# The end of a forward scan: weights issued early, six stores behind the rows, O and P in the V buffers, GLU buffers laid out anew

## The chip, the cores and the metric

The kernel runs as one program on one core of one Trainium2 chip. Five engines with queues of their own matter here: TensorE (PE; its weight loads are listed apart as PEld), VectorE (DVE), ScalarE (ACT), GpSimd (POOL) and SyncE (SP), which issues transfers only. Transfers are issued from queues too: SP's (SPq in the trace) and GpSimd's are those of interest. All of them are carried out by 16 DMA engines, between the memory outside (HBM) and the core's SBUF. The metric is the device time of one execution in microseconds (us); lower is better.

## The reference

One layer with two blocks under a condition vector, forward and backward: the output and eleven gradients. Block A is a recurrent attention, walked in 64 segments of 32 rows with 8 memory rows ahead of each; block B is a gated product. D is 512, there are 32 heads of 128, and F is 1792.

```python
for s in range(n_seg):                                   # 64 segments, one after the other
    h = concatenate([mem, xs], axis=1)                   # 8 + 32 rows
    q, k, v = (einsum('btd,dhe->bhte', h, W) for W in (Wq, Wk, Wv))
    p = softmax(where(mask, einsum('bhqe,bhke->bhqk', q, k) * scale, -1e9))
    o = einsum('bhqk,bhke->bhqe', p, v)
    o = einsum('bhte,hed->btd', o, Wo)
    mem = o[:, :M, :]; outs.append(o[:, M:, :])
...
x = x + ga * A(layernorm(x) * (1 + ca) + sa)
h = layernorm(x) * (1 + cb) + sb
x = x + gb * ((sigmoid(h @ w_gate) * (h @ w_up)) @ w_down)
```

## The kernel before

The program is a chain of passes: the forward scan over the 64 stages (segments), then a pass over the gated block (GLU) in 16 tiles of 128 rows, forward and backward at once, then weight gradients of the GLU, then the backward scan from stage 63 down to 0, last the weight gradients of the attention. All passes share one SBUF: a pool of a later pass lies over the buffers of an earlier one, and each first use of a buffer there waits for the last reader or writer of what lay beneath, a store's landing included.

**A stage of the forward scan** (`phase2`, lines 449 to 1163) makes K, Q and V rows (`proj`, `v_chunk`), turns them, makes the scores and their exponentials (`st_exp`, tile ET), the product with V (`pv`), and scales it by 1/sum into the tile Ost (`ost`, L957 on VectorE, L954 on ScalarE). Ost is turned into OT, OT times Wo gives the rows of the stage (`outproj`, at_ps); these are summed (`split_pair`, `sum_pair`) and stored to AOA in HBM by `store_rows` (L347), from GpSimd's queue. Each four stages the memory rows of four stages are worked out together by `TailRows` (ao_tps, ao_b) and stored in `rows_b` (L811). For the backward scan each stage also leaves in HBM: KST and QST (L608, L609), VT (L1154), PS (L1155, the scaled probabilities, tile Pst), OT (L1127) and OSR (L1089, from Ost); these go through SP's queue. ET, Vst and OT have two buffers, taken in turn; Ost, Pst and VTr have one.

**The last stage** (s = 63) has an order of its own. VT and PS are made on TensorE (`turn_v`, `turn_p`) rather than by a transposing transfer, PS is scaled in `scale_p` (L946, VectorE), and the work for tile 0 of the GLU runs in between in nine small steps (`first_tile`). The GLU's three weights are loaded over Wk and Wv from GpSimd's queue as those fall free: w_gate at L996, w_up at L1061, w_down at L1086. Rows of tile 1 are loaded at L995 (`glu_load`, L1188 to L1191), those of tile 0 at the end of the scan, then PS of stage 63 (L1160) and its K and Q rows (`late_rows`).

**The GLU pass** (`phase3`) is a pipeline of seven steps, s0 to s6, run deepest first, so that a tile's step k stands in turn k after the tile began. s0 makes the normed rows, s1 their turned form hdT, s2 gate and up products (L1333, L1337), their sigmoid and u (ScalarE), hh and umh (VectorE); s3 asks SP for the transpose hhT of hh (L1357) and makes du (L1364 on TensorE, L1366 on VectorE) and dg (L1368); s4 multiplies hhT with w_down (L1379); s5 multiplies the transposes of du and dg with the turned weights (L1404). In the first turns TensorE also turns w_down (L1242) and w_gate, w_up (L1231).

Order: every pass is recorded with `pin`, which keeps each engine's and queue's instructions in the order in which they are written; on SP and GpSimd in the scan, transfers stand in that order with the engine's own work. Buffers of the GLU come from the pool `p3s` in the order of their first use.

The edits touch `store_rows`, `rows_b`, `scale_p`, `ost`, `ott_first`, `ott_rest`, the body of the stage loop, its end, and the steps s0 to s5.

## Time and profile before

| | us |
|---|---|
| device time, median of 3 runs | 2972.12 |
| lowest and highest of them | 2970.28, 2975.39 |
| the profiled execution, its own time | 2976.26 |
| its span, first to last instruction | 2974.5 |
| GLU's gate products (L1333), first and last start | 952.1, 1240.4 |
| products with du's transpose (L1404) | 994.7 to 1274.2 |
| last gradient's products (L2300) | 2553.9 to 2971.0 |

All rows of the trace count from the start of the profiled span. TensorE is busy for 2913.0 us of it, 98%. The clock that was granted to it averaged 0.998.

How the views are read. The view of who waited for whom has one row for each pair of waiter and releaser: the sum in us, how often, and the longest. The view of busy time in stretches gives, after the stretch and its length, the busy us and the number of instructions of PE, PEld, DVE, ACT and POOL, then TensorE's clock, the busy share of the DMA engines and GB/s. The view in order of time gives start, length, engine, line, operation, tiles written and read, shapes and the number of merged instructions; in brackets the idle time before it and what ended it. SPq is SP's queue: a row there is the issue of a transfer, and its end is not the transfer's landing. A row in the view of one line gives shortest, median and longest duration in ns. In the view of transfers the last number of a row, where there is one, is the median time in us from issue to landing.

### The profile page before, as it was taken

Reading aid. Unit: us, or ns where it says so; the run is one execution under the profiler, and the core shown is the slowest. Engines: PE = TensorE matmul, PEld = TensorE weight load, DVE = VectorE, ACT = ScalarE, POOL = GpSimd, SP = SyncE. Lnnn points to the kernel's source line nnn. Section 1 sums busy time; section 2 is a strip of 40 time slices with the busy share of each in tenths; the row PEclk is TensorE's granted clock in tenths of the full one; section 3 lists DMA queues with packets and bytes.
Section 4 is the critical chain, followed back from the end, with each engine's and each line's share of the span. In section 5 each row is a group of like instructions: output and inputs, shape, how many; then the busy total and the mean of one; then the engine's idle time right before and its main releaser. Section 6 shows DMA issues by size and latency. Waiting matters only on the chain.

```text
span 2974.5 us, 105438 instructions
## 1 busy us (share of the span) xinstructions
PE 2913.0 (98%) x43838; PEld 1818.8 (61%) x43838; DVE 1625.0 (55%) x3689; ACT 1340.7 (45%) x3234; POOL 1231.7 (41%) x2487
## 2 busy tenths in 40 slices
PE   6999999999998999999999999999999999999999
PEld 3666666666665444445677776777777754445545
DVE  5565565665555788733456665666566632850011
ACT  3666666666665444312355555555555520110011
POOL 2555555545545222221344444444444432762111
PEclk9999999999999999999999999999999999999999
DMA  9889988998899899998699999999999997786565
GB/s 308 221 226 220 219 220 223 219 216 220 211 228 275 210 231 229 239 284 276 193 248 259 246 255 238 253 250 253 252 253 253 250 278 245 250 265 191 161 215 172
DMA packets 838066, 703.01 MB, mean 236 GB/s; under 512 B 537698, under 2 KB 710162, under 8 KB 836692
## 3 DMA queue, kind: packets, MB, share of 16 engines
q1 hardware_dynamic: 711972, 485.29, 66.3%
q0 software_dynamic: 54512, 148.63, 15.9%
q10 hardware_dynamic: 71104, 62.34, 6.5%
q8 instruction: 345, 5.65, 0.8%
q14 instruction: 133, 1.09, 0.1%
HBM read 294.99 MB, written 276.35 MB: 192 GB/s over the span
## 4 chain that ended last, share of the span: by engine, by line
PE 88%; DMA 4%; issue 3%; DVE 2%; ACT 1%; POOL 1%; SPq 0%; DVEq 0%; POOLq 0%; ACTq 0%
PE gps L2300 14%; PE pass_ps L257 14%; PE dh_ps L215 8%; PE g_ps L1923 5%; PE pass_ps L677 5%; PE gps5o L2315 4%; PE dhq_ps L223 4%; PE at_ps L223 4%; PE dh_tps L215 3%; PE gps L1583 3%; PE mm L1404 2%; PE turn_ps L890 2%; PE tps L1840 2%; PE st_ps L900 1%; PE mm L1364 1%
## 5 line engine op out<-in xcount | busy, mean ns | idle before, releaser
L2300 PE MATMUL gps<-rows,hrows 128*128 128x512 bf16 (+2 forms) x2160 | 415.5, 355 | 0.0
L2300 PEld LDWEIGHTS <-hrows 128*128 128x128 bf16 x2160 | 211.1, 98 | 204.5 <-issue 0.9
L1152 POOL TENSOR_TENSOR Pst<-Pst,rden 120x1408 bf16<-120x1408 bf16 x63 | 159.7, 2535 | 344.5 <-issue 209.0
L63 DVE CAST ot<-gps 128x512 bf16<-128x512 f32 (+3 forms) x76 | 48.1, 633 | 308.2 <-PE gps L2300 222.5
L1968 POOL COPY dOst<-RAd 96x512 bf16<-96x512 bf16 x128 | 75.1, 611 | 298.9 <-DVE RAd L63 298.7
L61 ACT ACTIVATE ot<-gps 128x512 bf16<-128x512 f32 (+3 forms) x75 | 41.2, 549 | 348.2 <-PE gps L2300 220.1
L677 PE MATMUL pass_ps<-Wv,hT 128*32 128x512 bf16 (+2 forms) x2304 | 186.8, 357 | 0.0
L2304 POOL DMA_DIRECT2D out_dram<-ot x104 | 78.6, 756 | 255.8 <-DVE ot L63 129.5
L257 PEld LDWEIGHTS <-hT 128*32 128x32 bf16 x4096 | 117.2, 97 | 95.9 <-issue 5.7
L63 DVE CAST Vst<-pass_ps 96x512 bf16<-96x512 f32 x128 | 87.3, 682 | 106.2 <-ACT RBv L61 102.7
L215 PE MATMUL dh_ps<-WvT,dVT 128*32 128x512 bf16 x2048 | 134.5, 383 | 1.7 <-DVE RBd L63 0.2
L223 PE MATMUL at_ps<-Wo,OT 128*32 128x256 bf16 x4096 | 128.1, 276 | 1.3 <-DMA Wo<-in_A_Wo_dram 0.9
L677 PE MATMUL pass_ps<-Wv,hb 128*32 128x512 bf16 (+2 forms) x636 | 126.5, 339 | 0.2
L257 PE MATMUL pass_ps<-Wk,hT 128*32 128x512 bf16 x2048 | 122.7, 380 | 2.1 <-POOL hT L563 1.1
L257 PE MATMUL pass_ps<-WoT,dyT 128*32 128x256 bf16 (+1 forms) x3072 | 122.8, 308 | 1.0 <-ACT dyT L2049 0.9
L257 PE MATMUL pass_ps<-Wq,hT 128*32 128x512 bf16 x2048 | 123.2, 379 | 0.3 <-DVE RBk L63 0.3
L223 PE MATMUL dhq_ps<-WqT,dQT 128*32 128x256 bf16 x4096 | 123.1, 273 | 0.2 <-issue 0.2
L215 PE MATMUL dh_ps<-WkT,dKT 128*32 128x512 bf16 x2048 | 122.3, 380 | 0.0
L2315 PE MATMUL gps5o<-WoT,rows 128*128 128x512 bf16 x560 | 121.0, 379 | 0.0
L223 PEld LDWEIGHTS <-dQT 128*32 128x32 bf16 x4096 | 109.9, 97 | 16.1 <-issue 0.4
L317 DVE TENSOR_TENSOR dST<-dh_ps,dST 128x512 bf16<-128x512 f32 x64 | 44.3, 692 | 130.3 <-ACT dST L316 130.3
L1910 DVE SCALAR_TENSOR_TENSOR dS<-dp_ps,Pst_l 128x480 bf16<-128x480 f32 (+1 forms) x192 | 106.2, 608 | 12.4 <-PE dp_ps L1908 6.7
(480 smaller groups left out, 7040.3 us busy)
## 6 DMA issues: line engine op xcount, KB each, us to landing
OSR<-Ost SPq DMA_DIRECT2D x64, 352.0 KB
OT<-OT SPq DMA_DIRECT2D x64, 352.0 KB
PS<-Pst SPq DMA_DIRECT2D x64, 352.0 KB
Pst_l<-PS SPq DMA_DIRECT2D x64, 352.0 KB
OT_l<-OT SPq DMA_DIRECT2D x64, 352.0 KB
DVR<-rows_x POOLq DMA_DIRECT2D x64, 352.0 KB, 6.0
DKR<-rows_x POOLq DMA_DIRECT2D x64, 352.0 KB, 5.7
DQR<-rows_x POOLq DMA_DIRECT2D x64, 352.0 KB, 3.5
```

The lines of the kernel that those rows point to most:

```text
L63: return nc.vector.tensor_copy(out, in_)
L215: self.nc.tensor.matmul(ps[32 * j:32 * j + 32, :], lhsT=lhsT, rhs=w, start=(n < 4), stop=(n >= total - 4), tile_position=(0, 32 * j))
L223: nc.tensor.matmul(ps[32 * j:32 * j + 32, :], lhsT=x[k], rhs=w[k][:, 256 * d:256 * d + 256], start=(n == 0), stop=(n == total - 1), tile_p ...
L257: self.nc.tensor.matmul(ps[32 * j:32 * j + 32, :], lhsT=lhs(c), rhs=rhs, start=(c == 0), stop=(c == DC - 1), tile_position=(0, 32 * j))
L677: nc.tensor.matmul(ps[32 * j:32 * j + 32, o * E:(o + n) * E], lhsT=lhsT, rhs=wc[:, 3 * a + hl:3 * (a + n - 1) + hl + 1:3, :], start=(c == ...
L1152: nc.gpsimd.tensor_tensor(Pst[0:120, :, :], Pst[0:120, :, :], rden[:, :].unsqueeze(2).to_broadcast([120, G, 128]), op=ALU.mult)
L1583: nc.tensor.matmul(ps[:], lhsT=h2r[:, j, c * 128:(c + 1) * 128], rhs=xr[:, j, :], start=(j == 0), stop=(j == NT - 1))
L1910: nc.vector.scalar_tensor_tensor(out=part3(dS, pi)[:, :, 0:120], in0=ps[:, 0:n, 0:120], scalar=cfg.scale, in1=part3(Pst, pi)[:, :, 0:120], ...
L1923: nc.tensor.matmul(ps[:, j, 0:w], lhsT=lh[:, g * GW:(g + 1) * GW], rhs=rh[:, g * GW:g * GW + w], start=True, stop=True)
L2300: nc.tensor.matmul(ps[:, 0:ng * E], lhsT=hrows[:, tp_, c * 128:(c + 1) * 128], rhs=rows[:, tp_, 0:ng * E], start=(tp_ == 0), stop=(tp_ == ...
L2304: (nc.sync if i == len(todo) - 1 else nc.gpsimd).dma_start(outw[c * 128:(c + 1) * 128, h0:h0 + 3 * (ng - 1) + 1:3, :], ot[:, 0:ng * E].rea ...
L2315: nc.tensor.matmul(pss[gg][:], lhsT=rows[:, t, gg * E:(gg + 1) * E], rhs=dyrows[:, t, :], start=(n == 0), stop=(n == NTP - 1))
```

## The change

- w_up is loaded right behind w_gate, ahead of the scaling of stage 62's Pst on GpSimd; w_down after the third V chunk.
- In stage 63, O is written into the free V buffer (`Orows`, that of the next stage, which does not exist) rather than Ost, and P into the stage's own V buffer, by ScalarE group by group (eleven small scalings with a per-row scale) rather than by three VectorE products.
- The stores of OSR, OT and PS of stages 62 and 63, and VT of 63, move behind the rows: `row_q` sends the last AOA rows through SP's queue, tiles 0 and 2 of the GLU are loaded next, and then the stores follow, in an order with `late_rows`' K and Q among them.
- The GLU's tiles are placed once in a fixed list before the pass (`places`, `buf`), so that the first buffer of each name has a chosen place; the number of buffers of each name stays the same.

```diff
+        self.row_q = nc.gpsimd
...
-                nc.gpsimd.dma_start(dram.rearrange("r (c x) -> (r c) x", x=128), rb[:])
+                self.row_q.dma_start(dram.rearrange("r (c x) -> (r c) x", x=128), rb[:])
...
-                    nc.gpsimd.dma_start(self.AOA[4 * b + i + 1, 32:32 + M, :].rearrange("r (c x) -> (r c) x", x=128),
+                    self.row_q.dma_start(self.AOA[4 * b + i + 1, 32:32 + M, :].rearrange("r (c x) -> (r c) x", x=128),
...
+                Orows = Ost if s < NS - 1 else Vsts[(s + 1) % 2]
...
                 def scale_p(pi):
-                    n = min(PG, G - pi * PG)
-                    nc.vector.tensor_tensor(Pst[0:120, pi * PG:pi * PG + n, :], turned_p[pi][0:120, 0:n, :],
-                                            rden[:, pi * PG:pi * PG + n].unsqueeze(2).to_broadcast([120, n, 128]), op=ALU.mult)
+                    for j in range(min(PG, G - pi * PG)):
+                        g = pi * PG + j
+                        nc.scalar.activation(Vst[0:120, g * GW:(g + 1) * GW], turned_p[pi][0:120, j, :], AF.Copy,
+                                             scale=rden[:, g:g + 1])
...
-                            nc.scalar.activation(Ost[0:120, g * GW:(g + 1) * GW], or_ps[0:120, j, :], AF.Copy,
+                            nc.scalar.activation(Orows[0:120, g * GW:(g + 1) * GW], or_ps[0:120, j, :], AF.Copy,
...
                     nc.gpsimd.dma_start(self.w_gate, io["B_w_gate"].rearrange("(c p) f -> p c f", p=128))
+                    nc.gpsimd.dma_start(self.w_up, io["B_w_up"].rearrange("(c p) f -> p c f", p=128))
...
                     v_chunk(s, 2)
                     first_tile[5]()
+                    nc.gpsimd.dma_start(self.w_down, io["B_w_down"].rearrange("(fc p) d -> p fc d", p=128))
...
-                else:
-                    nc.gpsimd.dma_start(self.w_up, io["B_w_up"].rearrange("(c p) f -> p c f", p=128))
...
-                if s == NS - 1:
-                    nc.gpsimd.dma_start(self.w_down, io["B_w_down"].rearrange("(fc p) d -> p fc d", p=128))
-                    for g0, t, w in ((0, RAs[0]["k"], 8), (8, RAs[0]["q"], G - 8)):
-                        nc.sync.dma_start(self.VT[s, :, g0:g0 + w, :], t[:, 0:w * GW].rearrange("p (g x) -> p g x", x=GW))
-                nc.sync.dma_start(self.OSR[s], gl3(Ost))
+                if s < NS - 2:
+                    nc.sync.dma_start(self.OSR[s], gl3(Ost))
                 at_ps = outproj()
                 if s == NS - 1:
-                    nc.sync.dma_start(self.OT[s], gl3(OT))
...
                     parts = self.split_pair(sb2, at_ps, "at")
+                    scale_p(2)
...
+                    self.row_q = nc.sync
                     self.pop_later()
+                    scale_p(0)
                     self.pop_later()
                     turn_p(1)
+                    scale_p(1)
                     self.pop_later()
-                    for pi in (2, 0, 1):
-                        scale_p(pi)
+                    self.row_q = nc.gpsimd
                     break
...
-                nc.sync.dma_start(self.OT[s], gl3(OT))
+                if s < NS - 2:
+                    nc.sync.dma_start(self.OT[s], gl3(OT))
...
-                    nc.sync.dma_start(self.PS[s], Pst[:])
+                    if s < NS - 2:
+                        nc.sync.dma_start(self.PS[s], Pst[:])
...
-            self.glu_first[0] = self.glu_load(0, nc.sync)
-            nc.sync.dma_start(self.PS[NS - 1], Pst[:])
+            for j in (0, 2):
+                self.glu_first[j] = self.glu_load(j, nc.sync)
+            for g0, t, w in ((0, RAs[0]["k"], 8), (8, RAs[0]["q"], G - 8)):
+                nc.sync.dma_start(self.VT[NS - 1, :, g0:g0 + w, :], t[:, 0:w * GW].rearrange("p (g x) -> p g x", x=GW))
+            nc.sync.dma_start(self.OT[NS - 1], gl3(OTs[(NS - 1) % 2]))
+            nc.sync.dma_start(self.OSR[NS - 1], gl3(Vsts[NS % 2]))
+            nc.sync.dma_start(self.PS[NS - 1], gl3(Vsts[(NS - 1) % 2]))
+            nc.sync.dma_start(self.OSR[NS - 2], gl3(Ost))
             late_rows()
+            nc.sync.dma_start(self.OT[NS - 2], gl3(OTs[NS % 2]))
+            nc.sync.dma_start(self.PS[NS - 2], Pst[:])
...
+            places = (("f32tmp", [128, D], F32, 5), ("u", [128, F], BF16, 1), ("sg", [128, F], BF16, 2),
+                      ("h2", [128, D], BF16, 2), ("db", [128, D], BF16, 2), ("xh2", [128, D], BF16, 5), ("x1", [128, D], F32, 4),
+                      ("hhT", [128, FC, 128], BF16, 1), ("duT", [128, FC, 128], BF16, 1), ("du", [128, F], BF16, 2),
+                      ("dgT", [128, FC, 128], BF16, 1), ("dg", [128, F], BF16, 2), ("hh", [128, F], BF16, 2),
+                      ("umh", [128, F], BF16, 1), ("hdT", [128, 2 * DC, 128], BF16, 2))
+            first_of = {t: sbp.tile(shape, dt, name=t, tag=t, bufs=n) for t, shape, dt, n in places}
+
+            def buf(name, tag=None):
+                tag = tag or name
+                _, shape, dt, n = next(p for p in places if p[0] == tag)
+                return first_of.pop(tag, None) or sbp.tile(shape, dt, name=name, tag=tag, bufs=n)
...
-                hhT = sbp.tile([128, FC, 128], BF16, name="hhT", bufs=1)
+                hhT = buf("hhT")
```

In s0 to s5 every other tile of the list is taken by `buf` in the same way.

More of the change, by code (lines that the diff above doesn't have):

```diff
@@ L966, in ott_rest @@
                     for g in range(PG, G):
-                        nc.tensor.transpose(ps[:, g - PG, 0:120], Ost[0:120, g * GW:(g + 1) * GW], self.ident[0:120, 0:120])
+                        nc.tensor.transpose(ps[:, g - PG, 0:120], Orows[0:120, g * GW:(g + 1) * GW], self.ident[0:120, 0:120])
                     for pi in (1, 2):
@@ L1300, in s1 @@
                     return st
-                hdT = sbp.tile([128, 2 * DC, 128], BF16, name="hdT", bufs=2)
+                hdT = buf("hdT")
                 if j == 1:
@@ L1324, in s2 @@
                 hdT = st["hdT"]
-                u = sbp.tile([128, F], BF16, name="u", bufs=1)
-                sg = sbp.tile([128, F], BF16, name="sg", bufs=2)
-                hh = sbp.tile([128, F], BF16, name="hh", bufs=2)
-                umh = sbp.tile([128, F], BF16, name="umh", bufs=1)
+                u = buf("u")
+                sg = buf("sg")
+                hh = buf("hh")
+                umh = buf("umh")
                 for ch in range(NCH):
@@ L1387, in out @@
                 def out():
-                    t1 = sbp.tile([128, D], F32, name="t1", tag="f32tmp", bufs=5)
+                    t1 = buf("t1", "f32tmp")
                     nc.vector.tensor_tensor(t1[:], b_bf[:], gb_bc[:], op=ALU.mult)
@@ L1410, in s5 @@
                 nc.scalar.activation(dh2b[:], hp[:], AF.Copy)
-                dxh = sbp.tile([128, D], F32, name="dxh", tag="f32tmp", bufs=5)
+                dxh = buf("dxh", "f32tmp")
                 s1_ = sbp.tile([128, 1], F32, name="s1", bufs=2)
@@ L1416, in s5 @@
                 nc.vector.tensor_tensor(pr2[:], hp[:], xh2[:], op=ALU.mult)
-                junk = sbp.tile([128, D], F32, name="junk", tag="f32tmp", bufs=5)
+                junk = buf("junk", "f32tmp")
                 s2_ = sbp.tile([128, 1], F32, name="s2", bufs=2)
@@ L1510, in after @@
                         wd_products(fc, parts[fc], [NT - 1, *range(NA, NT - 2)])
-                        wd_chunk(fc, parts[fc], sbp.tile([128, D], BF16, name="ot2", tag="h2", bufs=2))
+                        wd_chunk(fc, parts[fc], buf("ot2", "h2"))
                 if it == NT + 3:
```

30 lines of the change are left out of this document (15 added, 15 removed).

## The prediction

> **What bounds the kernel now.** The page comes first, then who waited on TensorE around the end of the forward pass, then the busy time there in stretches of 3.41 us (the step in which the granted clock changes in this trace), last the order of time on each engine and queue.
>
> ```profile
> span 2974.5 us, 105438 instructions
> ```
>
> ```profile
> PE mm L1379 <- DMA hhT<-hh: 3.1, 1, 3.1
> PE tps L918 <- DVE Ost L957: 1.7, 3, 0.9
> PE or_ps L906 <- DVE rden L911: 1.6, 1, 1.6
> ...
> PE tp L1242 <- DMA Wv<-in_B_w_down_dram: 1.1, 1, 1.1
> ```
>
> ```profile
> 940.53:943.95 3.42, 1.75 (x24) 1.25 (x23) 2.40 (x8) 1.14 (x4) 1.38 (x2) 1.00 0.97 292
> 943.95:947.36 3.41, 3.22 (x65) 2.36 (x68) 1.58 (x4) 2.42 (x4) 2.82 (x5) 0.50 0.94 339
> ...
> 954.19:957.60 3.41, 3.41 (x20) 1.76 (x18) 3.19 (x7) 2.38 (x5) 0.47 (x2) 1.00 1.03 402
> 957.60:961.01 3.41, 2.28 (x32) 1.72 (x30) 2.66 (x4) 2.00 (x4) 1.85 (x3) 1.00 0.90 313
> ...
> 974.67:978.08 3.41, 0.34 (x2) 0.21 (x3) 1.18 (x2) 1.40 (x3) 1.12 (x2) 1.00 0.80 231
> 978.08:981.49 3.41, 3.41 (x27) 2.65 (x25) 0.69 (x1) 0.83 (x1) 0.00 (x0) 0.50 0.66 147
> ```
>
> ```profile
> 1020.00:1040.00 20.00, 20.00 (x105) 9.62 (x104) 17.62 (x32) 7.46 (x13) 5.64 (x11) 1.00 0.89 227
> ```
>
> The second number is TensorE's busy time, the third from the end its clock, the last two DMA share and GB/s. From about 1000 us on TensorE is full (20.00 of 20.00), so only the seam between the passes can give time. It holds four waits. Two of them also cost clock: after a stretch with 1.75 us of work the next ran at 0.50, after one with 0.34 too, after one with 2.28 not.
>
> ```profile
> 926.75 1.94 PE L223 MATMUL at_ps<-Wo,OT 128*32 128x256 bf16 x64
> ...
> 942.91 0.38 PE L918 MATMUL tps<-ident,Ost 120*128 120x120 bf16 x4 [0.95 <-DVE Ost L957]
> ...
> 944.17 3.46 PE L223 MATMUL at_ps<-Wo,OT 128*32 128x256 bf16 x64 [0.19 <-DVE OT L63]
> ...
> 952.14 0.92 PE L1333 MATMUL mm<-Wk,Wq 128*128 128x448 bf16 x4 [0.32 <-DVE ao_b_rb L343]
> ...
> 959.49 0.96 PE L1242 MATMUL tp<-ident,Wv 128*128 128x128 bf16 x14 [1.13 <-DMA Wv<-in_B_w_down_dram]
> ...
> 977.75 0.75 PE L1379 MATMUL mm<-Wv,hhT 128*128 128x512 bf16 x2 [3.08 <-DMA hhT<-hh]
> ```
>
> The wait that ends last is that for hhT, the transpose of GLU tile 0: TensorE was ready at 977.75 - 3.08 = 974.67. Whatever is saved before it only lengthens this wait, unless hhT itself lands earlier. **The forecast is therefore made from the SP queue, which issues hhT.**
>
> ```profile
> 930.22 1.99 SPq L1059 DMA_TRANSPOSE Pst<-ET  x1
> 932.30 0.95 SPq L1089 DMA_DIRECT2D OSR<-Ost  x1
> ...
> 942.06 0.34 SPq L1154 DMA_DIRECT2D VT<-VTr  x1
> ...
> 962.10 0.68 SPq L1188 DMA_DIRECT2D Wv<-in_A_x_dram  x1
> ...
> 969.60 3.05 SPq L1357 DMA_TRANSPOSE hhT<-hh  x1
> ```
>
> ```profile
> SPq L1154 <- DMA OSR<-Ost: 4.2, 1, 4.2
> SPq L1190 <- DMA VT<-VTr: 3.0, 1, 3.0
> ```
>
> The store of VT reads VTr, yet it waited for OSR, which stands eight issues before it: an SP issue waits until the eighth DMA before it has landed. OSR took 942.06 - 932.30 = 9.8 us beside the weight load. hhT took 977.75 - 969.60 = 8.15 us from issue to use.
>
> **The change part by part.** (1) *O of stage 63 goes to the free V buffer.* Ost was still being stored for stage 62:
>
> ```profile
> 942.16 0.69 DVE L957 TENSOR_TENSOR Ost<-or_ps,rden 120x512 bf16<-120x512 f32 x1 [0.99 <-DMA OSR<-Ost]
> ...
> 951.41 0.22 DVE L343 COPY at_rb<-at_tp 128x128 bf16<-128x128 bf16 x1
> ...
> 953.31 1.75 DVE L946 TENSOR_TENSOR Pst<-pt_ps,rden 120x384 bf16<-120x384 bf16 x3 [1.22 <-DMA PS<-Pst]
> 954.98 0.68 DVE L1266 TENSOR_TENSOR t<-Wk,Wv 128x512 f32<-128x512 bf16 x1
> ...
> 960.49 0.68 DVE L1292 TENSOR_TENSOR db<-Wk,Wv 128x512 bf16<-128x512 bf16 x1
> ...
> 965.80 2.58 DVE L1366 TENSOR_TENSOR du<-mm,sg 128x448 bf16<-128x448 f32 x4
> ```
>
> ```profile
> 942.15 1.14 ACT L954 ACTIVATE Ost<-or_ps,rden 120x128 bf16<-120x128 f32 x4 [2.89 <-DMA OSR<-Ost]
> ...
> 953.15 0.54 ACT L1334 ACTIVATE sg<-mm 128x448 bf16<-128x448 f32 x1 [2.18 <-PE mm L1333]
> ```
>
> TensorE gains its 0.95. The stretch 940.53 to 943.95 then holds 1.75 + 0.95 = 2.70 us of work, more than the 2.28 that kept the clock, so at_ps should take 1.94 instead of 3.46: 1.52 more. The last copies at_rb and the first GLU product come 0.95 + 1.52 = 2.47 earlier; I take 2.4, as ScalarE has a table load in between. The wait of 1.6 for rden stays, nothing before it changes. If the half clock stays, only 0.95 is left.
>
> The Trainium skill, "TensorE: Matmul & The Clock Gate", section "The HAM clock gate", says that the clock falls after a whole idle window of about 3.4 us. The trace disagrees: a window with 1.75 us of work was enough. By that rule the 1.52 would have no tie to this wait; then it stays, and the end gains 1.0 instead of 2.5.
>
> (2) *P of stage 63 by ScalarE into the other V buffer.* Three VectorE scalings (1.75) and their wait for PS (1.22) go; eleven of 1.14 / 4 = 0.285 us come. Three lie behind the 1.89 us of tail products, eight (2.28) fall where ScalarE idled 2.18 before the first sigmoid: 0.10 late, covered by five PSUM buffers; uncovered it would be 2.28. VectorE, whose last row copy released the product at 952.14, starts tile 1 at 952.14 - 2.4 = 949.7 instead of 954.98 and ends db at 961.17 - 5.3 = 955.9, as the w_down transposes begin.
>
> (3) *w_up and w_down early.*
>
> ```profile
> 932.06 0.78 POOL L996 DMA_DIRECT2D Wk<-in_B_w_gate_dram  x1
> 936.74 2.53 POOL L1152 TENSOR_TENSOR Pst<-Pst,rden 120x1408 bf16<-120x1408 bf16 x1 [3.90 <-issue]
> ...
> 941.08 0.82 POOL L1061 DMA_DIRECT2D Wk<-in_B_w_up_dram  x1
> ...
> 945.09 1.10 POOL L1086 DMA_DIRECT2D Wv<-in_B_w_down_dram  x1
> ```
>
> ```profile
> Wk<-in_B_w_up_dram POOLq DMA_DIRECT2D x1, 1792.0 KB, 11.7
> ...
> OSR<-Ost SPq DMA_DIRECT2D x2, 352.0 KB
> ```
>
> w_up is issued at 932.9, right behind w_gate, and w_down takes w_up's old place, 941.1. POOL's queue loses 0.8 us before the Pst scaling, which idled 3.90 anyway. Three weights are 5.5 MB; with 0.75 MB of rows and VT at the 402 GB/s of the row at 954.19 they take 15.5 us: even counted only from 936.74, when the Pst transpose is in, w_up is there at 947.7 and w_down at 952.2. Before, six stores of 0.36 MB shared that time. They are needed later: w_up just after the first GLU product, now 949.7, w_down 958.36 - 952.14 = 6.2 later, 955.9. So the wait of 1.13 goes; were w_down no earlier than 959.49, it would be 3.5 long. TensorE now reaches hhT 2.4 + 1.13 = 3.5 earlier, at 971.1.
>
> (4) *Rows before stores on SP.* at_rb (ready at 951.63 - 2.4 = 949.2) and all behind it now stand in SP's queue. From it to hhT stand 34 issues: at_rb and four tail rows (from GpSimd's queue), 11 loads of tiles 0 and 2, eight big stores in VT, OT, OSR, PS, OSR, OT, PS order, four of KST and QST between, 6 loads.
>
> ```profile
> L1190 SPq DMA_DIRECT2D Wv<-AOA x52: 303/431/1318, 945.9 to 1182.9; - x52
> ```
>
> Price of one, from both sides: 0.43 (median) + 0.09 to the next (932.21 to 932.30 above) = 0.52; and (969.60 - 962.10) / 12 = 0.625 in the last free-running stretch, which ends with one slow issue. I take 0.55, nearer the many rows: 18.7 us, hhT issued at 967.9 (966.9 to 970.5) against 969.60. Until use: 6.5 (the Pst transpose, 930.22 to 936.74) to 8.15; I take 7.3, as w_down is gone but the stores' tail lies ahead of it. TensorE goes on at 975.2 (973.4 to 978.6): **2.5 us earlier.** It still idles 971.1 to 975.2, so the second half-clock stretch stays.
>
> (5) *GLU buffers.* Tile 0's first buffers no longer lie over stored tiles, but du now lies over OT and RA0k, dg over RA1q, hhT over the V buffer and Ost. New waits: VectorE's du (965.80 - 3.5 = 962.3) for OT, issued as the 19th at 949.2 + 18 x 0.55 = 959.1. Its landing I take as 4 us: the block holds seven stores' worth, 2.5 MB, 6.3 us at 402 GB/s, and is issued over 12 x 0.55 = 6.6, so no queue builds up (the bound is the 9.8 above). That makes du 0.8 late. Behind it stand dg and tile 2's chain, and TensorE's tile 1 waits for the PSUM buffers that du reads; all of it is covered by the 4.1 us that TensorE idles for hhT.
>
> **Sum.** 2974.5 - 2.5 = 2972.0 span; the profiled execution's own time 2976.26 becomes 2973.8. The median of the runs, 2972.12, lies 4.1 below that execution; carried over: **2969.6**. Own range of this case: gain 4.4 to loss 0.9, and 1.5 later if the half clock at 944 stays: 2967.7 to 2974.5.
>
> **Rivals.** *A: the wait for hhT vanishes.* With the weights gone by 952, SP issues at its floor, 0.303 + 0.09: hhT after 13.4 us at 962.6, plus 6.5 = 969.1, before 971.1. Then 977.75 - 971.1 = 6.65 and half of the 3.41 us at half clock, 1.7: 2963.8. For it: the DMA engines have nothing big to do from 952 to 957. Against: the median issue is 0.43, and the stores still lie just ahead. *B: the eight-deep wait.* hhT waits for OT of stage 62, eight before it, and that for OT of stage 63, eight before again: hhT not before 959.1 + 2 L, L a store's landing. With the 9.8 us of OSR: 978.7, used at 986.0, 8.3 us later: 2980.4. It decides from L = 5.7 on, and costs 5.9 from L = 8.6. For it: SP's rows show exactly this wait; against: that 9.8 was beside a weight load of 1792 KB. *C: nothing comes of it.* w_up stood behind w_gate on its queue anyway, the half clock at 944 stays, at_rb is 1.5 later and hhT lands as before: 2972.1.
>
> **Chances.** Forecast 0.46, A 0.33, B 0.12, C 0.09. 0.2% is 5.9 us, about what a measurement of this kernel can tell from no change. Faster: A and a tail of the forecast, 0.34; slower: B, 0.12; same: the rest, 0.54. Range to hold 8 in 10: 2963.0 (A in) to 2975.5, B left out.
>
> **What would show it.** Right: no wait of TensorE for Ost and w_down; at_ps near 1.9 us at clock 1.00; hhT issued near 968 on SP, TensorE's L1379 row (now the only large wait) resuming near 975 with about 4 us of idle. Wrong: hhT issued before 964 or its wait gone (A); SP's issues in the store block waiting on OT and OSR for several us each (B); a changed rate anywhere after 1000 us would show that I missed a cause.

## The result, and the profile after

| | before | after |
|---|---|---|
| median of 7 runs, us | 2972.12 | 2982.67 |
| lowest and highest, us | 2970.28, 2976.64 | 2978.13, 2989.30 |
| the profiled execution, own time, us | 2976.26 | 2986.17 |
| its span, us | 2974.5 | 2984.4 |

Ratio 1.0034, with a 95% interval of 1.0022 to 1.0046: some 10 us slower, where 2969.6 was forecast (2963.0 to 2975.5). Timed again on another chip, the kernel before took 2975.67 and the changed one 2984.76, ratio 1.0029 (1.0019 to 1.0039).

Who waited for whom in the profile after, TensorE and VectorE from 930 to 1000 us:

```profile
PE mm L1403 <- DMA hhT<-hh: 7.3, 1, 7.3
PE or_ps L908 <- DVE rden L913: 2.5, 1, 2.5
...
DVE dg L1392 <- DMA QST<-RA1q: 6.3, 1, 6.3
```

The waits for stage 63's Ost and for w_down are gone, as forecast. The wait for hhT is not shorter but has grown from 3.1 to 7.3 us. VectorE's wait for QST is new: dg of tile 0 now lies over rows that are still being stored. TensorE in order of time:

```profile
931.29 1.94 PE L224 MATMUL at_ps<-Wo,OT 128*32 128x256 bf16 x64
...
949.07 3.60 PE L224 MATMUL at_ps<-Wo,OT 128*32 128x256 bf16 x64
957.19 0.92 PE L1357 MATMUL mm<-Wk,Wq 128*128 128x448 bf16 x4 [0.32 <-DVE ao_b_rb L344]
985.57 1.04 PE L1403 MATMUL mm<-Wv,hhT 128*128 128x512 bf16 x2 [7.33 <-DMA hhT<-hh]
1002.98 0.81 PE L1428 MATMUL mm<-Wq,duT 128*128 128x512 bf16 x3
```

Stage 62's output product, which no edit to stage 63 can reach, started at 931.29 rather than 926.75: 4.5 us of the lag were there before the seam began. So from here on times in the seam are counted from that product. hhT was used 985.57 - 931.29 = 54.3 us after it (51.0 before), the first product with duT came after 71.7 us (994.70 - 926.75 = 67.95 before). SP's queue in the same profile (issue, length, transfer):

```profile
956.71 0.32 SPq L348 DMA_DIRECT2D AOA<-at_rb  x1
...
965.04 0.45 SPq L1166 DMA_DIRECT2D VT<-RA0k  x1
...
967.71 1.18 SPq L1170 DMA_DIRECT2D OSR<-Ost  x1
...
971.30 1.78 SPq L609 DMA_DIRECT2D QST<-RA1q  x1
...
973.61 1.63 SPq L1172 DMA_DIRECT2D OT<-OT  x1
...
979.67 2.73 SPq L1381 DMA_TRANSPOSE hhT<-hh  x1
```

From at_rb to hhT it is 979.67 - 956.71 = 22.96 us for the 34 issues, 0.675 each where 0.55 was taken. The first 16 took 8.33 us, 0.52 each; the 18 from the first VT store on took 14.63, 0.81 each. The slow ones begin a little later still: the first five stores took 0.44 to 0.47 us each, and from the sixth (OSR from Ost, 967.71) single issues took up to 1.78.

### The profile page after: what moved, and what is told of

It is laid out like the page before. It is cut to its first block, busy times and chain, and to the rows that moved or that the text cites. A ratio compares the mean times of both kernels' runs of the same rounds, so it can differ in the third digit from the quotient of the medians.

```text
span 2984.4 us, 105445 instructions
## 1 busy us (share of the span) xinstructions
PE 2918.9 (98%) x43838; PEld 1824.5 (61%) x43838; DVE 1626.2 (54%) x3686; ACT 1344.7 (45%) x3245; POOL 1231.8 (41%) x2482
## 4 chain that ended last, share of the span: by engine, by line
PE 63%; DMA 2%; DVE 1%; issue 1%; ACT 1%; SPq 1%; POOL 0%; DVEq 0%; ACTq 0%; POOLq 0%
PE gps L2324 14%; PE dh_ps L216 8%; PE g_ps L1947 5%; PE pass_ps L258 5%; PE gps5o L2339 4%; PE dhq_ps L224 4%; PE mm L1428 3%; PE gps L1607 3%; PE dh_tps L216 3%; PE mm L1403 2%; PE mm L1388 2%; PE tps L1864 1%; PE mm L1357 1%; PE mm L1361 1%; PE gps L1506 1%; PE dp_ps L1924 1%
```

## The experiments

Parts of the change were undone or done alone, and two more profiles were taken of each unaltered kernel. The runs were made on several chips, each beside the kernel before on the same chip, so the ratios are what compares. "Seam" below is the time from the start of stage 62's output product to the first product with duT.

Theories for the first four runs: **Q**, hhT is late because 34 issues stand on SP behind a wait for at_rb; **W**, the weights loaded together delay stage 62's Pst, hence rden, and bring a second half-clock stretch.

**Rows back on GpSimd.**

```diff
-                    self.row_q = nc.sync
```

> The changed kernel with the rows at_rb and ao_b of stage 63 stored from GpSimd's queue again, all else as changed; SP no longer waits for at_rb before the loads and stores. Theory Q (the SP queue: hhT is late because 34 issues stand behind the wait for at_rb, and those from the stores on took 0.81 us each rather than 0.52): SP starts its loads and stores several us earlier, hhT is issued at least 4 us earlier against the start of stage 63, and the time falls by 5 to 9 us, to 2974 to 2978. Theory W (the weights loaded together delay stage 62's Pst and with it rden of stage 63, and a second half-clock stretch follows): the wait for rden stays at 2.5, no gain above 2 us, 2981 to 2983.

2970.10 against 2969.76, ratio 1.0000 (0.9989 to 1.0010). The loss is gone with this one line (and the one that sets the queue back). The changed kernel itself was executed only once on this chip; the variant with the weights late, below, was timed beside this one and has the loss there. TensorE and SP in its profile:

```profile
931.32 1.94 PE L224 MATMUL at_ps<-Wo,OT 128*32 128x256 bf16 x64
...
977.25 0.39 PE L1401 MATMUL mm<-Wv,hhT 128*128 128x512 bf16 x1 [3.64 <-DMA hhT<-hh]
...
992.66 0.81 PE L1426 MATMUL mm<-Wq,duT 128*128 128x512 bf16 x2
```

```profile
971.93 3.29 SPq L1379 DMA_TRANSPOSE hhT<-hh  x1
```

hhT is issued 40.6 us after the reference point, not 48.4 (44.1 and 45.1 in the two later profiles of the changed kernel), and used after 45.9; the seam takes 61.3. The first store of VT was handed over at 955.66, 24.3 us after the reference point; in the profile after it was 965.04 - 931.29 = 33.8. Theory Q said 2974 to 2978, a ratio of 1.0006 to 1.0020: right in direction, too small in size. Theory W's 2981 to 2983 is far off, and the wait for rden is absent here although the weights are early.

**The stores back at their old places** (VT, OT, OSR of 63 and OSR, OT, PS of 62; the diff shows one of them).

```diff
-                if s < NS - 2:
-                    nc.sync.dma_start(self.OSR[s], gl3(Ost))
+                nc.sync.dma_start(self.OSR[s], gl3(Orows))
```

> The changed kernel with five of the six late stores (VT, OT, OSR of stage 63, OSR, OT and PS of stage 62; only PS of stage 63 still at the end) back at their old places, O and P still in the V buffers, rows still on SP, weights early. Theory Q: 28 issues rather than 34 behind at_rb, none of them throttled by seven big stores: 28 x 0.52 = 14.6 us, hhT issued 8 us earlier after at_rb than in the changed kernel, its wait nearly gone, 2973 to 2976. Theory W: the stores are not the cause and now share the memory with the weights again: 2982 or more.

2974.81, ratio 1.0019 (1.0008 to 1.0030). A part of the loss is gone, not all. hhT was issued 21.8 us after at_rb, where Q said 14.6, but not because the issues were long: the 27 of them took 13.1 us, 0.49 each. SP's waits in this profile:

```profile
SPq L348 <- DVE at_rb L344: 4.8, 1, 4.8
SPq L812 <- DMA PS<-Pst: 1.8, 1, 1.8
SPq L812 <- DMA VT<-RA0k: 1.8, 1, 1.8
```

SP was held for 4.8 us at at_rb, and behind it waited for the landings of the stores ahead. With 1.5 for the other VT store and 1.3 for OSR that is 6.4 us in four waits, each for the transfer eight before: the wait of rival B, in a kernel where the stores stand ahead. Its hhT was used 46.9 us after the reference point, earlier than on the mean of the kernel before (47.8). The seam of 67.2 has another wait in it: 3.2 us of TensorE for VectorE's copies of w_gate's turns, which stand behind a wait of dg for QST of 5.7. (The expectation counts five stores moved back; the list in it has six, and PS of 63 stood at the end before the change too.)

**w_up and w_down late again.**

```diff
-                    nc.gpsimd.dma_start(self.w_up, io["B_w_up"].rearrange("(c p) f -> p c f", p=128))
                     norms.pop()()
```

> The changed kernel with w_up and w_down issued at their old places (w_up after the second denominator, w_down ahead of the output product). Theory Q: TensorE arrives at hhT about 1 us later or earlier, the hhT wait takes it up, the time stays at 2981 to 2984. Theory W: the wait for rden falls from 2.5 to about 1.6 us, one half-clock stretch of 3.41 us (1.7 us) goes, 2978 to 2980.

2978.53, ratio 1.0028 (1.0019 to 1.0037). In us that is W's forecast; as a ratio it lies between W's (1.0020 to 1.0027) and Q's (1.0030 to 1.0040), so the time does not separate the two. What it shows is that nearly all of the loss is there without the early weights. hhT came 23.3 us after at_rb and TensorE waited 7.3 us for it, as in the changed kernel. The wait for rden was absent in this profile, but it was absent in the next one too, where the weights are early.

**The changed kernel once more.**

> The changed kernel unaltered, for a second profile. Theory Q: against the start of stage 63's K pass (834.83 + 100 = 934.83 us in the first profile) at_rb is issued on SP 21.9 us later, hhT 44.8 us later, and TensorE resumes with it 50.7 us later, each within 1 us. That the scan reached stage 63 4.5 us later than in the profile before is either chance of the execution (then this profile shows another offset, between 0 and 5 us) or belongs to the change (then 4 to 5 us again).

One time, 2972.97, below every other time of this kernel (2978.13 to 2991.68, on other chips). at_rb on SP 20.8 us, hhT 44.1 and its use 49.9 us after stage 62's product, a wait for hhT of 7.6 us, no wait for rden, seam 67.8. Counted from the start of the K pass, Q's three forecasts (21.9, 44.8 and 50.7) came out 4 to 5 us too late, because at_rb was early; from at_rb to hhT it was 23.3 us again. Stage 62's product came at 924.4, not at 931.3: the 4.5 us were chance.

That asked for the kernel before again; theory **E** was that the loss lies behind the seam.

> The kernel before unaltered, for a second profile. Five profiles so far reached stage 62's output product at 924.4 to 931.3 us, and lose 1.2 to 1.8 us at single places that differ from profile to profile. Theory Q (the change costs in the seam alone): the time from stage 62's output product to the first product with duT is 68 us again within 1 us (67.95 in the first profile). Theory E (elsewhere: the backward scan runs quieter in the kernel before): from there to the end 1976 us again, against 1979 to 1982 in the profiles of the changed kernel.

> As the run before it: theory Q 68 us within 1 us for the seam, with 1976 to 1982 behind it by chance; theory E 1976 within 1 us behind it once more.

2972.85 and 2976.59. Their seams took 61.1 and 64.6 us against the 67.95 of the profile on which the forecast stood. TensorE and SP in the first of the two:

```profile
933.29 1.94 PE L223 MATMUL at_ps<-Wo,OT 128*32 128x256 bf16 x64
...
955.26 0.92 PE L1333 MATMUL mm<-Wk,Wq 128*128 128x448 bf16 x4 [0.31 <-DVE ao_b_rb L343]
963.31 0.95 PE L1242 MATMUL tp<-ident,Wv 128*128 128x128 bf16 x14 [1.70 <-DMA Wv<-in_B_w_down_dram]
...
994.43 0.81 PE L1404 MATMUL mm<-Wq,duT 128*128 128x512 bf16 x3
```

```profile
969.02 2.86 SPq L1357 DMA_TRANSPOSE hhT<-hh  x1
```

Here TensorE waited neither for hhT nor for stage 63's Ost nor for rden; of the prediction's waits only w_down's is there. In the third it waited 2.16 us for hhT. **The wait for Ost and the half clock at 944, on which step (1) rested, and the wait for rden were those of one execution.** Q had said 68 us for the seam and missed twice. Behind the seam the three profiles of before ran 1979.8, 1976.6 and 1975.5 us, the first with a stall of some 4 us near 1834; E had said 1976 there, and it came out twice.

> The changed kernel unaltered, timed beside the kernel before on this chip, with a third profile. Theory Q: the time is 2976 to 2981, ratio 1.002 to 1.004; the seam (stage 62's output product to the first product with duT) takes 67.8 to 71.7 us, and hhT is issued on SP 23 us after at_rb. Theory E: seam not longer than before on the mean, the excess of 5 to 10 us behind it.

2984.76 against 2975.67, ratio 1.0029 (1.0019 to 1.0039). Seam 67.9, hhT 22.7 us after at_rb, as Q has it. But behind the seam it ran 1981.6 us, and the other two profiles of the changed kernel 1981.4 and 1979.0, as E has it, though E had the seam unchanged: each theory finds a part of the loss. SP's waits and TensorE's rows in this profile:

```profile
SPq L348 <- DVE at_rb L344: 12.2, 1, 12.2
```

```profile
928.20 1.94 PE L224 MATMUL at_ps<-Wo,OT 128*32 128x256 bf16 x64
...
979.24 1.03 PE L1403 MATMUL mm<-Wv,hhT 128*128 128x512 bf16 x2 [7.15 <-DMA hhT<-hh]
...
996.11 0.81 PE L1428 MATMUL mm<-Wq,duT 128*128 128x512 bf16 x3
```

SP stood still for 12.2 us at at_rb, until 950.55. From there to 958.88 it handed over at_rb, the tail rows and the loads, and only then the first of the stores:

```profile
958.88 0.46 SPq L1166 DMA_DIRECT2D VT<-RA0k  x1
```

What that does to the memory is seen in the busy time in stretches of 5 us (the last two numbers are DMA share and GB/s), first of the kernel before in its second profile, then of the changed one:

```profile
950.00:955.00 5.00, 4.08 (x70) 2.42 (x67) 2.02 (x6) 2.20 (x5) 4.35 (x8) 1.00 1.01 396
955.00:960.00 5.00, 4.74 (x25) 2.32 (x25) 4.18 (x9) 2.72 (x5) 3.26 (x7) 1.00 1.04 403
960.00:965.00 5.00, 3.31 (x40) 2.32 (x39) 3.44 (x5) 2.72 (x5) 2.32 (x4) 1.00 1.04 368
965.00:970.00 5.00, 4.89 (x64) 3.81 (x62) 4.57 (x7) 5.00 (x6) 0.54 (x1) 1.00 0.58 169
```

```profile
950.00:955.00 5.00, 4.65 (x27) 2.50 (x28) 3.77 (x10) 4.11 (x12) 0.85 (x4) 1.00 0.77 248
955.00:960.00 5.00, 5.00 (x64) 3.99 (x63) 3.78 (x6) 4.35 (x7) 2.28 (x3) 1.00 0.54 157
960.00:965.00 5.00, 4.85 (x49) 3.21 (x47) 4.67 (x7) 3.85 (x5) 0.54 (x1) 1.00 1.01 376
965.00:970.00 5.00, 5.00 (x28) 2.62 (x27) 0.67 (x2) 2.72 (x5) 0.54 (x1) 1.00 0.96 295
```

Before, the DMA engines are full until 965 and free when hhT is asked for at 969.0. Changed, they are full under the hold too, with the weights (1.01 from 945 to 950), but 0.77 and 0.54 busy from 950 to 960, while SP hands over the small transfers ahead of the stores, and full again from 960 on. That is the stretch in which hhT waits its turn behind the stores (issued at 973.28). The stores are the same; they come after the hold rather than under it.

**The layout undone** (buffers in the order of first use again).

```diff
-            first_of = {t: sbp.tile(shape, dt, name=t, tag=t, bufs=n) for t, shape, dt, n in places}
+            first_of = {}
```

> The changed kernel with the buffers of the gated block placed in the order of their first use, as before (the table of places left out); stores, rows, weights, O and P as changed. Now hh, du, dg and hhT wait for the late stores of stages 62 and 63. Theory Q: the stores, which SP issues only after at_rb, now hold VectorE's first products too: hhT is issued no earlier, 2982 to 2990. Theory E: as the changed kernel, 2976 to 2981.

2986.10, ratio 1.0031 (1.0020 to 1.0043). The time is that of the changed kernel, and in us it is Q's; but its loss lies at another place. TensorE doesn't wait for hhT at all; it waits before the GLU's own products:

```profile
PE mm L1361 <- ACT sg L1358: 10.3, 1, 10.3
```

ScalarE's first sg stood for 12.7 us until the store of OSR had landed, which lies beneath it in the old layout. hh was ready only 44.8 us after the reference point, and hhT was issued at once. So the new layout does take tile 0's first products off the late stores, as it was meant to; with the stores late on SP that only moves the wait to hhT. Theories Q and E were not told apart by it.

The next three ask whether it is the **hold (H)** or the number of issues and the stores just ahead of hhT **(N)**.

**The rows on SP, behind fifteen others.** The loads of tiles 0 and 2 and the stores of VT, OT and OSR of stage 63 are written ahead of `store_rows`:

```diff
+                    for j in (0, 2):
+                        self.glu_first[j] = self.glu_load(j, nc.sync)
...
                     self.store_rows(psp, sb2, ft, self.AOA[s + 1, 0:32, :], "at", "p")
                     self.row_q = nc.sync
```

> The changed kernel with the loads of tiles 0 and 2 and the stores of VT, OT and OSR of stage 63 (15 issues) written ahead of the rows at_rb and ao_b, which stay on SP. Theory H (SP held: everything behind at_rb starts only when the last row copy is done): 15 issues of 0.5 to 0.8 us now run while SP would wait, hhT is issued 8 to 11 us earlier after at_rb, 13 us rather than 23, and the time is within 0.1% of before, ratio 0.999 to 1.001. Theory N (not the hold but the five more issues on SP, or the big stores just ahead of hhT): the same number of issues and stores, hhT 20 us or more after at_rb, ratio 1.002 to 1.004.

2972.16, ratio 1.0005 (0.9997 to 1.0014), theory H. at_rb was now issued 28.7 us after stage 62's product (its copy was done at 20.7), hhT after 42.7, its use after 48.0.

**The rows on SP alone, in the kernel before.**

```diff
                     self.store_rows(psp, sb2, ft, self.AOA[s + 1, 0:32, :], "at", "p")
+                    self.row_q = nc.sync
```

> The kernel before with one part of the change alone: at_rb and ao_b of stage 63 stored from SP rather than GpSimd. Behind them in SP's order stand only the loads of tile 0, PS of stage 63, four K and Q rows and the loads of tiles 2 and 3; the big stores stay ahead. Theory H: the hold alone makes hhT late, as with the stores at their old places (21.8 us after at_rb there), ratio 1.002 to 1.003. Theory N: without the stores behind it the hold is harmless, ratio 0.999 to 1.001.

2972.88, ratio 1.0009 (0.9999 to 1.0018): N's forecast, not H's. hhT was issued 20.4 us after at_rb, but its wait was 1.9, and SP's hold at at_rb 4.6 us rather than 12.2, as its stores were ahead. A short hold with the stores ahead costs little here, and late stores without a hold (rows back on GpSimd, 1.0000) cost nothing: the loss takes a hold with the stores behind it. That reading joins H and N, and was made after these runs. The 1.0019 with the stores at their old places, at a hold of 4.8 us, fits it only in part.

**Rows and stores both undone.** What is left are the early weights, O and P in the V buffers, and the layout.

> The changed kernel with the rows on GpSimd's queue and five of the six stores at their old places: what is left are the weights issued early, O and P in the V buffers, and the layout. Theory H: SP isn't held and has fewer transfers left behind at_rb, hhT issued at 36 to 40 us after stage 62's output product, no wait for it, ratio 0.998 to 1.000. Theory N: 0.998 to 1.000 too; if the weights beside the stores cost something it shows here as 1.001 or more.

2972.08, ratio 1.0007 (0.9998 to 1.0017): these parts bring no gain that can be measured, against the 0.998 to 1.000 that both theories forecast. hhT was issued after 39.6 us, as H has it, but TensorE still waited 3.45 us for it.

One thing more stood between the stores and hhT in every kernel: six loads for tiles 5 and 6, written for later turns and put forward, because SP's order is pinned for the first four turns only. **Theory I**: the end follows hhT's issue; **J**: something else sets it.

```diff
-                if it == 4:
+                if it == 6:
                     self.pin(i0, [ET.SP])
```

> The changed kernel with the loads of the first six turns kept in their written order on SP, which puts six loads of tiles 5 and 6 (AOA x4 and two of the output's gradient) behind hhT of tile 0 rather than ahead of it. Theory I (the end follows hhT's issue): hhT is issued 3.6 us earlier, 19 us after at_rb rather than 23, TensorE's wait falls from 7.3 to about 4, and the ratio to before from 1.003 to 1.0015 to 1.002. Theory J (hhT's issue isn't what sets the end; the du and dg chain or the memory does): 1.0025 to 1.0035 as the changed kernel.

2974.95, ratio 1.0015 (1.0005 to 1.0024): I's forecast, at its edge. Its rows on SP, TensorE and VectorE:

```profile
950.12 0.32 SPq L348 DMA_DIRECT2D AOA<-at_rb  x1
...
969.38 2.72 SPq L1381 DMA_TRANSPOSE hhT<-hh  x1
```

```profile
975.30 0.94 PE L1403 MATMUL mm<-Wv,hhT 128*128 128x512 bf16 x2 [3.65 <-DMA hhT<-hh]
978.71 1.01 PE L1243 MATMUL tp<-ident,Wk 128*128 128x128 bf16 x8 [2.47 <-DVE Wq L63]
```

```profile
971.22 1.09 DVE L1392 TENSOR_TENSOR dg<-du,umh 128x1792 bf16<-128x1792 bf16 x1 [5.85 <-DMA QST<-RA1q]
```

hhT came 969.38 - 950.12 = 19.3 us after at_rb, its wait halved. The seam, 67.3 us, is hardly shorter. A second chain seems to take the gain there: dg waits for QST, VectorE is late with the copies of w_gate's turns, and TensorE waits 2.47 us for them.

> The same with the rows on GpSimd's queue, where TensorE still waited 3.64 us for hhT. Theory I: that wait goes, 3.6 us and half of one or two half-clock stretches less than without the edit, ratio 0.998 to 0.999. Theory J: 1.000 within 0.001.

2970.68, ratio 1.0005 (0.9996 to 1.0014): theory I missed, J held. SP and TensorE there:

```profile
962.71 6.06 SPq L1379 DMA_TRANSPOSE hhT<-hh  x1
```

```profile
927.06 1.94 PE L224 MATMUL at_ps<-Wo,OT 128*32 128x256 bf16 x64
...
972.56 0.60 PE L1401 MATMUL mm<-Wv,hhT 128*128 128x512 bf16 x2 [3.20 <-DMA hhT<-hh]
```

hhT was issued 35.7 us after the reference point, 5 us earlier than with the rows on GpSimd and no pin, but its issue alone lasted 6.06 us, and it was used after 45.5, hardly earlier than 45.9. TensorE waited 3.20 us for it, so that use is the landing: here an earlier issue was no earlier landing.

> The kernel before with the six loads behind hhT and nothing else changed; its wait for hhT was 3.08, 0 and 2.16 us in three profiles. Theory I: 1.7 us less on the mean, ratio 0.999 to 0.9997. Theory J: 1.000 within 0.0005.

> The changed kernel with the rows on GpSimd's queue, five stores at their old places and the six loads behind hhT: of the change, the early weights, O and P in the V buffers and the layout are left. Its wait for hhT was 3.45 without the last edit. Theory I: 3 to 5 us less than without it, ratio 0.9985 to 0.9995. Theory J: 1.000 to 1.001.

2970.70, ratio 1.0002 (0.9993 to 1.0011), and 2973.49, ratio 1.0008 (1.0000 to 1.0017): no gain either, as J has it. In the first TensorE didn't wait for hhT, and SP had no queue left ahead of it: hh was ready 36.2 us after the reference point and hhT was issued after 36.3. In the second TensorE didn't wait for hhT but 4.06 us for VectorE's copies, behind a wait of dg for QST of 3.29.

The last three ask what dg's wait costs by itself (**K**): the four K and Q stores are written ahead of the big ones.

```diff
+            late_rows()
...
             nc.sync.dma_start(self.OSR[NS - 2], gl3(Ost))
-            late_rows()
```

> The changed kernel with the four K and Q row stores of stage 63 written ahead of the six big stores, right behind the loads of tiles 0 and 2; the number of issues ahead of hhT is the same. VectorE's dg (in the changed kernel 5.6 us late for QST) waits under 2 us. Theory I (hhT's issue sets the end, dg's wait is covered by hhT's): the ratio stays at 1.002 to 1.0035. Theory K (dg's wait is a cost of its own): 1.001 to 1.002.

> The same edit in the kernel with the six loads behind hhT (1.0015 without the edit; its turns of w_gate waited 2.47 us for VectorE). Theory K: that wait goes, ratio 1.0005 to 1.001. Theory I: 1.0015 again, 1.001 to 1.002.

> The same two edits with the rows on GpSimd's queue: no hold of SP, hhT behind fewer issues, dg without its wait; of the changed kernel's costs none is left that the traces show. Both theories: 0.9985 to 1.000; 1.0005 or more would mean a cost that no trace has shown yet.

Ratios 1.0010 (0.9999 to 1.0021), 1.0014 (1.0003 to 1.0025) and 0.9998 (0.9988 to 1.0009). VectorE in the first of them:

```profile
969.60 1.09 DVE L1392 TENSOR_TENSOR dg<-du,umh 128x1792 bf16<-128x1792 bf16 x1
```

dg's wait is gone, and the time is K's. But its profile still has 7.86 us of wait for hhT and a seam of 69.6, so it doesn't show where the gain lies. The second run has the six loads behind hhT too; there TensorE's wait for VectorE's copies is gone, as K said, and the time is I's all the same. Whether dg's wait is a cost of its own stays open. The third, rows on GpSimd with both edits, equals the kernel before; no version here beats it by more than the measurement tells.

The profiles together, in us from the start of stage 62's output product (read from rows such as those shown; each is one execution):

| kernel | hhT issued | hhT used | seam | time ratio |
|---|---|---|---|---|
| before, three profiles | 42.9, 35.7, 40.3 | 51.0, 44.8, 47.6 | 68.0, 61.1, 64.6 | 1 |
| after, three profiles | 48.4, 44.1, 45.1 | 54.3, 49.9, 51.0 | 71.7, 67.8, 67.9 | 1.0034, 1.0029 |
| layout undone | 44.8 | 54.6 | 70.9 | 1.0031 |
| weights late | 44.8 | 50.4 | 68.5 | 1.0028 |
| stores early | 42.5 | 46.9 | 67.2 | 1.0019 |
| after, six loads behind hhT | 41.5 | 47.4 | 67.3 | 1.0015 |
| rows alone | 41.9 | 47.8 | 63.2 | 1.0009 |
| rows behind fifteen | 42.7 | 48.0 | 65.2 | 1.0005 |
| rows on GpSimd | 40.6 | 45.9 | 61.3 | 1.0000 |
| rows on GpSimd, stores early | 39.6 | 45.7 | 63.9 | 1.0007 |
| the same, six loads behind hhT | 38.1 | 45.6 | 66.4 | 1.0008 |
| rows on GpSimd, six loads behind hhT | 35.7 | 45.5 | 62.4 | 1.0005 |
| before, six loads behind hhT | 36.3 | 46.0 | 62.4 | 1.0002 |
| after, K and Q stores first | 46.2 | 52.8 | 69.6 | 1.0010 |
| the same, six loads behind hhT | 45.0 | 55.5 | 72.5 | 1.0014 |
| rows on GpSimd, both edits | 35.6 | 45.5 | 62.5 | 0.9998 |

In the altered kernels the time is that of before within 0.1% where the seam took 61 to 66.4 us, and 1.0010 to 1.0034 of it where it took 67 to 73. The order within the second group isn't that of the ratios, and the first profile of before, with 68.0, would fall in it: one execution stands here for seven to twelve.

## Why the prediction was wrong

**The base.** The sum started from one profile, and that profile's seam of 67.95 us was the longest of three. The prediction noted that its execution lay 4.1 us above the median, and subtracted that as a constant; a part of it lay in the seam itself. So the gains of step (1) were gains against waits that are mostly not there: stage 63's output product ran at full clock (1.93 us) in the second and third profile of before and in two of after's three. The first GLU product came 22.0 us after stage 62's in those two profiles of before and 25.9, 21.2 and 22.8 in after's: 0.7 earlier at best, not 2.4. In after's first profile rden was 2.5 us late and the half clock lasted two steps (at_ps 3.60).

**Step (2)** held: no wait on the P scalings shows in after's profiles. **Step (3)** was right that w_down's wait goes (1.1 and 1.7 us in two of before's profiles, in none of after's). But with step (1) it brings less than 2 us, not 3.5: TensorE is ready for hhT (use less wait) 47.0, 42.3 and 43.9 us after the reference point, 44.4 on the mean, against 47.9, 44.8 and 45.5, 46.1 on the mean, before. That moves the start of the wait for hhT and nothing else, as the prediction said.

**Step (4) is where the sum failed, and it was the price of an issue.** The forecast was at_rb 22.4 us after stage 62's product (949.2 - 926.75), 18.7 for 34 issues, 7.3 until use: 48.4. The means of after's three profiles are 22.8, 23.0 and 5.9: 51.7. The first term was good on the mean (25.4, 20.8 and 22.4 singly, so in part by luck), the last 1.4 too long; the middle one was 4.3 too short. The 0.55 came from queues in which loads stand, and for the first 16 issues, rows and loads, 0.52 was right; the 18 from the first store on took 0.81. The range allowed 0.52 to 0.625. In rows that the prediction quoted, OSR's issue took 0.95 us (at 932.30) and the slowest load of L1190 1.318, so slow issues were there to be seen. Against its own base that makes 0.7 us of loss instead of 2.5 of gain; against the mean of the three profiles of before (47.8) it is 3.9 later.

What the step also lacked was the other side of the hold. It counted at_rb as the start of the queue, but not that before the change SP used those 11.3 to 14.5 us to hand over the stores. The runs show this is the cause: one line that takes the rows off SP brings 1.0029 to 1.0034 down to 1.0000, and rows that stay on SP behind fifteen others, four of them the stores of VT, OT and OSR, come to 1.0005.

**Step (5)** named dg over RA1q and priced only du's wait for OT. du's wait was 0.6 us at most in after's profiles, near the 0.8 forecast; dg's wait for QST was 6.3, 6.0 and 5.6 us. Its price remains open (above).

**Rivals.** A counted on idle DMA engines and on 0.39 us an issue. The engines are half idle from 955 to 960 (0.54), but the issues took 0.52, and the stores come ahead of hhT. B gave 2980.4, the nearest time, but by luck: SP's waits in the third profile of after hold no wait for a store's landing, only the 12.2 us for at_rb; the issues themselves are long. B's waits do occur with the stores at their old places (above). C did not occur.

**What stays open.** The seam grew from a mean of 64.6 to one of 69.1 us, 4.6 of the 9 to 11 that the runs show; against the two calmer profiles of before (62.9) it is 6.3. Most of it is TensorE standing still: 9.1, 5.3 and 7.0 us of the seam before, 11.9, 10.2 and 10.9 after, 3.8 more on the mean. Theory E is not excluded for the rest: behind the seam it is 1977.3 us on the mean before and 1980.7 after, 3.4 more. But the parts outside the seam differ from execution to execution by more than that (stage 62's product at 924.4 to 934.7 us in these six; behind the seam 1984.0 us in the profile of the rows alone, whose ratio is 1.0009), so the last 3 to 6 us are not placed. The wait for rden shows in five of the eight profiles with rows on SP and the stores behind them, in one of three of before, and in no profile of another variant. Where it shows, GpSimd began to scale stage 62's Pst 9.8 to 12.2 us after the reference point, elsewhere 6.1 to 7.8; no run ties it to one edit.

**The clock.** The prediction's rule was that a step of 3.41 us with 1.75 us of work drops the clock and one with 2.28 keeps it. Busy time of the changed kernel in such steps, first profile (second number TensorE's, third from the end the clock):

```profile
942.33:945.74 3.41, 1.69 (x30) 1.34 (x28) 0.38 (x1) 1.47 (x5) 2.99 (x2) 1.00 1.04 385
945.74:949.15 3.41, 2.41 (x28) 2.22 (x31) 2.92 (x9) 1.17 (x5) 1.72 (x2) 0.50 1.01 374
949.15:952.56 3.41, 3.41 (x68) 2.52 (x72) 1.52 (x3) 2.39 (x4) 2.82 (x5) 0.50 1.02 383
```

1.69 us of work dropped it, as the rule has it; but once at half, 2.41 us of work didn't bring it back, and the step after, full to its end, still ran at half. So a late wait can cost two steps, not one. The rows below are from the rows alone, then from the rows on GpSimd with the six loads behind hhT.

```profile
946.52:949.93 3.41, 2.10 (x19) 0.96 (x16) 3.17 (x9) 1.19 (x2) 0.95 (x2) 1.00 1.01 409
949.93:953.34 3.41, 2.70 (x8) 1.14 (x9) 2.51 (x7) 0.54 (x1) 0.58 (x1) 0.50 1.03 408
```

```profile
1274.16:1277.57 3.41, 1.62 (x9) 0.54 (x8) 3.18 (x10) 0.81 (x1) 0.51 (x1) 1.00 0.56 184
1277.57:1280.99 3.42, 3.22 (x20) 1.58 (x21) 1.72 (x3) 1.08 (x2) 2.69 (x6) 1.00 0.76 201
```

A step with 2.10 us of work dropped the clock there, and one with 1.62 kept it. So the prediction's rule is not one: TensorE's busy time alone doesn't decide the fall, and what does stays open. The Trainium skill, "TensorE: Matmul & The Clock Gate", section "The HAM clock gate", has the clock fall after a whole idle window of about 3.4 us and rise after a busy one of that length: the first three rows agree with its rise and again disagree with its fall.

## What to carry to other kernels

A transfer that waits for a late result had better not stand ahead of bulk transfers on the same queue: here the bulk lost the time under the wait and came out just ahead of the next urgent transfer, and the repair was one line, another queue for the waiting one. Price an issue from rows with the same transfers ahead of it on its queue: ahead of the stores an issue took 0.52 us on the mean, behind the first of them 0.81. And before costing waits of a microsecond, take two or three profiles of the kernel before: the seam here ran 61 to 68 us in the same program, and the wait for Ost and the half clock behind it were in one of three.

## What was not expected of the hardware

The same store is handed over in 0.32 us or in 1.18, with the DMA engines equally full. The first of KST in the second profile of before (DMA share 1.04 around it), and in the third of after (1.01):

```profile
957.79 0.32 SPq L608 DMA_DIRECT2D KST<-RA1k  x1
```

```profile
962.67 1.18 SPq L609 DMA_DIRECT2D KST<-RA1k  x1
```

So a full memory alone doesn't make an issue long. Before, SP had waited 4.0 us for the landing of an earlier store (VT) just ahead, for PS at 956.89; after, it had handed over six stores in the 3.8 us before, without waiting for a landing. In both SP's queue is slow behind the stores, once by waiting and once by long issues; why it is the one here and the other there was not tested.

A transfer asked for earlier need not land earlier. In two of the three kernels with the rows on GpSimd and the six loads behind hhT, TensorE waited for hhT, so that its use is its landing: issued after 35.7 and 35.6 us it was used after 45.5, where the rows on GpSimd alone had 40.6 and 45.9. Its issue took 6.1 and 4.4 us there, 1.7 to 3.8 in all other profiles. The memory around it in the first of the two:

```profile
960.00:965.00 5.00, 5.00 (x28) 2.62 (x27) 2.81 (x5) 2.49 (x5) 0.72 (x2) 1.00 0.98 316
965.00:970.00 5.00, 4.36 (x35) 2.54 (x32) 4.13 (x8) 1.52 (x4) 1.10 (x2) 1.00 1.10 187
```

The DMA engines are full in both. The Trainium skill, "DMA: Bandwidth & Descriptors", section "Queues, rings and completion order", says that each DMA engine takes the descriptors of one issuing queue in their order. These rows fit that, with the last two stores handed over just ahead of hhT, at 960.73 and 961.35; they don't show it by themselves. hhT from another queue was not tried.

Executions of one program differ by whole stalls: the first profile of before lost some 4 us near 1834 that the other two didn't, and stage 62's product came between 924.4 and 934.7 us in the six profiles of the two kernels, with the same work ahead of it.
